# Batch 1's rest ahead of batch 0's main, loads in two column halves from SP's queue, later weight blocks

## The chip, the cores and the metric

The kernel runs on one core of a Trainium2 chip. The metric is the device time of one execution in microseconds (us), lower is better. TensorE is called PE here, VectorE DVE, ScalarE ACT, GpSimd POOL, SyncE SP; PEld is PE's weight load.

## What is computed

A long convolution of 12480 tokens by 128 channels, and two layers of a feed-forward network with 2048 hidden channels behind it, all in float32:

```python
h_filt = (np.maximum(pos_emb @ w1, 0.0) @ w2) * np.exp(-0.01 * pos)[:, None]
u = x * v
y = np.fft.irfft(np.fft.rfft(u, n=2*S, axis=1) * np.fft.rfft(h_filt, n=2*S, axis=0), n=2*S, axis=1)[:, :S]
a = x * y
h = a @ w_in;  a = (h * np.clip(h + 3, 0, 6) / 6) @ w_out        # first layer
h = a @ w_in2; out = where(h > 0, h, exp(min(h, 0)) - 1) @ w_out2 # second layer
```

The four weight matrices arrive as 64-bit floats.

## The kernel before

**Stages.** The convolution is a two-stage Fourier transform written as matrix products, in four steps: `first` (over token blocks), `second` (per frequency, with the product by the filter), `third_main` and `third_rest` (back along one axis) and `fourth` (back along the other, into tokens). The two layers follow as one long stream, called step five here. Every instruction is issued in the order in which the program text calls it, each engine runs its own in that order, and pools and semaphores only add waits; no scheduler moves anything.

**Step three** ends with `third_main(0, ...)`, nine pieces of the main frequencies of channel half 0 (seven of 8 channels, two of 4). For each piece PE makes `q` (L495), ACT copies half of it (L510), DVE adds and subtracts it into `main` (L501). All nine must have left DVE before a matmul of step four may read `main`.

**Step four** has 17 batches (`BATCHES`). `fourth(i, y)` multiplies in two parts: `most` reads `main`, `rest` reads `own` and `other`, which are complete since before `third_main(0, ...)`. Batch 0 has half as many matmuls as the others. Even batches do rest, then most; odd ones most, then rest. DVE then multiplies the result by the signal (L728, L731). Each batch needs a table `ti` (294 KB, six slots, so that batch i+6's is loaded by `load_ti` once batch i has left PE) and a piece of the signal `xT` (`load_x`), brought by SP's DMA queue. `behind` makes a load wait for the last ACT instruction that was noted in `paced`.

**The weights' conversion** runs beside all this. `weight_steps` is a generator of 32 jobs of 256 columns: load 64-bit words (L261), rebuild 32-bit floats with ACT (L271, L272), DVE (L283 to L286) and POOL (L289), and store to `w_scratch` (L266, on ACT's queue). A job's load is issued two steps ahead. In steps one and two the loads go out on SP's queue; `queue[0] = nc.scalar` moves them to ACT's queue from step three on. `convert(RATE[..])` advances the generator at a fractional rate: 0.45 per piece of `third_main(0, ...)`, 0.55 per batch of step four, and `convert(1000)` does what is left after the last batch.

**Step five** reads the converted weights back as 16 blocks of 512 columns, `W[i, q]` (L707), and splits each in two (`split_w`: ACT L711, then POOL or DVE L712) at the unit that `pieces` names. Three blocks are loaded during the last batches of step four, the other 13 in one go after it. A unit n multiplies one 256-column part of the hidden layer for one tile of 512 tokens: `mm1` (L807) makes h in one of three PSUM buffers, ACT activates (L817 or L819), DVE gates (L828 or L830), ACT and DVE split the result (L836, L841), and `mm2` (L851) adds it to the accumulator `acc[m]`, whose buffer has the tag `o1` or `o2` by the layer m. Every unit has 12 PE matmuls; the first layer runs alone for 13 units.

## Time and profile before

| what | value |
|---|---|
| median of 3 timed runs | 1328.4 us (1328.37 to 1329.41) |
| the profiled execution's own time | 1326.08 us |
| its span, first to last instruction | 1324.3 us |
| PE busy in the span | 1313.1 us (99%) |
| DVE, ACT, POOL busy | 1137.3, 1005.5, 406.0 us |
| TensorE's granted clock | 1.000 of full speed |
| start of step four on PE, start of step five on PE | 213.63 us, 252.90 us |

The first five rows are from the list of times and the head of the profile page, the last from the timeline. The span is counted from the first instruction; the profiled execution's own time is 1.8 us longer than its span, for what lies around it. PE is the bound by its share alone, so what can be saved is the time in which it stands still, or work that it does twice.

### The profile page before, as it was taken

To read this page: it belongs to the slowest core of one execution; us is meant where nothing else is said; L and a number is where in the kernel's file an instruction comes from. 1 tells how busy PE (TensorE), PEld (TensorE's weight loads), DVE (VectorE), ACT (ScalarE), POOL (GpSimd) and SP (SyncE) were. 2 spreads that over 40 slices of the span, in tenths; PEclk is the share of its full clock that TensorE was granted. 3 is DMA by queue.
4 is the path that set the end of the run, shared out by engine and by line. 5 is a ranking of instruction groups with operands and counts; after the bars stand their busy time and mean duration, and the time that the engine had idled before them with its cause. 6 is when DMAs were issued, how large, how long until landed. Compare 5 with 4: busy or idle time off the path is not lost.

```text
span 1324.3 us, 22981 instructions
## 1 busy us (share of the span) xinstructions
PE 1313.1 (99%) x9184; PEld 1127.5 (85%) x9184; DVE 1137.3 (86%) x1213; ACT 1005.5 (76%) x1210; POOL 406.0 (31%) x302
## 2 busy tenths in 40 slices
PE   9999999999999999999999999999999999999998
PEld 9999999878888888888888888888888888888898
DVE  6769877699988888888888888888888888898897
ACT  5677663488878887788878887788778878887776
POOL 1027741214222322222233322222222233322223
PEclk9999999999999999999999999999999999999999
DMA  8945338700000000000000000000000000000000
GB/s 271 267 126 160 108 103 273 230 22 1 9 8 1 9 8 8 1 9 8 9 9 0 9 9 8 0 9 8 9 1 9 8 9 1 8 8 9 8 8 13
DMA packets 33676, 58.80 MB, mean 44 GB/s; under 512 B 3962, under 2 KB 10272, under 8 KB 33568
## 3 DMA queue, kind: packets, MB, share of 16 engines
q1 hardware_dynamic: 27232, 50.18, 12.2%
q10 hardware_dynamic: 6336, 7.15, 1.6%
q8 instruction: 72, 1.18, 0.4%
q14 instruction: 36, 0.29, 0.1%
HBM read 46.73 MB, written 10.58 MB: 43 GB/s over the span
## 4 chain that ended last, share of the span: by engine, by line
PE 92%; DVE 3%; ACT 1%; issue 1%; DMA 1%; POOL 0%; SPq 0%; ACTq 0%; DVEq 0%; POOLq 0%
PE o L851 38%; PE h L807 38%; PE pa L395 4%; PE y L651 3%; PE z L467 2%; PE q L495 2%; PE r L448 1%; DVE gs L841 1%; PE h L457 1%; PE pr L349 1%; PE q L531 1%; DVE g L828 1%; DMA cv<-in_mw 0%; DMA w_scratch<-cv 0%; DVE g L830 0%
## 5 line engine op out<-in xcount | busy, mean ns | idle before, releaser
L851 PE MATMUL o<-gs,w 128*128 128x512 f32 (+1 forms) x2400 | 566.0, 384 | 0.7 <-DVE gs L841 0.4
L851 PEld LDWEIGHTS o<-gs,w 128*128 128x128 f32 x2400 | 445.0, 188 | 86.6 <-ACT y L780 0.8
L820 POOL TENSOR_SCALAR a<-a 128x1024 f32<-128x1024 f32 (+1 forms) x200 | 296.2, 1481 | 713.0 <-ACT a L819 712.9
L841 DVE TENSOR_TENSOR gs<-g,gs 128x1024 fp32r<-128x1024 f32 (+1 forms) x400 | 482.8, 1207 | 4.4 <-ACT gs L836 3.4
L836 ACT CAST gs<-g 128x1024 fp32r<-128x1024 f32 (+1 forms) x400 | 410.1, 1025 | 55.0 <-DVE g L828 53.4
L828 DVE SCALAR_TENSOR_TENSOR g<-a,h 128x1024 f32<-128x1024 f32 (+1 forms) x200 | 238.6, 1194 | 114.6 <-ACT a L817 114.6
L807 PE MATMUL h<-xs,w 128*128 128x512 f32 (+1 forms) x1200 | 298.2, 384 | 2.2 <-DVE g L828 2.2
L807 PE MATMUL h<-x,w 128*128 128x512 f32 (+1 forms) x1200 | 298.1, 384 | 0.2 <-DVE g L830 0.2
L819 ACT ACTIVATE a<-h 128x1024 f32<-128x1024 f32 (+1 forms) x200 | 201.3, 1007 | 90.3 <-PE h L807 89.2
L807 PEld LDWEIGHTS h<-xs,w 128*128 128x128 f32 x1200 | 223.1, 188 | 47.4 <-DVE g L828 3.3
L807 PEld LDWEIGHTS h<-x,w 128*128 128x128 f32 x1200 | 223.1, 188 | 43.8 <-ACT gs L836 0.5
L817 ACT ACTIVATE a<-h,bounds 128x1024 f32<-128x1024 f32 (+1 forms) x200 | 218.8, 1094 | 47.6 <-PE h L807 47.3
L830 DVE SCALAR_TENSOR_TENSOR g<-a,h 128x1024 f32<-128x1024 f32 (+1 forms) x200 | 237.4, 1187 | 0.2 <-POOL a L820 0.2
L289 POOL TENSOR_TENSOR cv<-cv 128x256 int32<-128x256 int32 x32 | 23.4, 732 | 126.3 <-DVE cv L286 118.2
L395 PE MATMUL pa<-tab,qb 98*64 98x180 f32 x512 | 41.6, 316 | 0.0
L395 PEld LDWEIGHTS pa<-tab,qb 98*64 98x64 f32 x512 | 37.7, 138 | 2.4
L271 ACT ACTIVATE cv<-cv 128x256 int32<-128x256 uint32 x32 | 14.2, 444 | 22.6 <-DMA cv<-in_mw 18.1
L712 POOL TENSOR_TENSOR w<-w 128x512 fp32r<-128x512 f32 x12 | 17.1, 1436 | 38.4 <-ACT w L711 38.4
L486 POOL TENSOR_TENSOR qb<-qb,bp 128x1024 f32<-128x1024 f32 (+1 forms) x12 | 26.9, 2244 | 3.9 <-DVE bp L481 3.9
L783 ACT COPY y<-o 128x512 f32<-128x512 f32 (+1 forms) x25 | 14.4, 577 | 17.5 <-PE o L851 17.5
L486 POOL TENSOR_TENSOR au<-qb,au 128x1024 f32<-128x1024 f32 (+1 forms) x12 | 26.9, 2242 | 0.5 <-DVE au L481 0.5
L651 PE MATMUL y<-qb 128*64 128x97 f32 (+3 forms) x688 | 24.6, 248 | 0.0
(97 smaller groups left out, 874.5 us busy)
## 6 DMA issues: line engine op xcount, KB each, us to landing
uv<-in_xc SPq DMA_DIRECT2D x32, 196.0 KB
out_T<-y SPq DMA_DIRECT2D x23, 256.0 KB
qb<-in_gm SPq DMA_DIRECT2D x22, 256.0 KB
cv<-in_mw SPq DMA_DIRECT2D x21, 256.0 KB
au<-in_xT SPq DMA_DIRECT2D x16, 268.0 KB
w_scratch<-cv ACTq DMA_DIRECT2D x32, 128.0 KB
w<-w_scratch SPq DMA_DIRECT2D x16, 256.0 KB
cv<-in_vc SPq DMA_DIRECT2D x20, 196.0 KB
```

Of the source, the lines that this page charges most:

```text
L395: nc.tensor.matmul(pa[f * HN:(f + 1) * HN, j, :2 * NK], lhsT=src(j, f), rhs=table[:, f], start=True, stop=True)
L486: nc.gpsimd.tensor_tensor(out=spectrum(hf, k0 + a, n), in0=m1, in1=m2[:, :, :, ::-1], op=ALU.add)
L651: nc.tensor.matmul(y[c * HD:(c + 1) * HD, b, off:off + w], lhsT=lhsT, rhs=rhs[:, H1 - w:], start=(b, c) in fresh, stop=done, skip_group_ch ...
L807: nc.tensor.matmul(h[:, j], lhsT=wslice(2 * m - 2, a, 2 * u + j), rhs=x[:, b], start=i == 0, stop=i == 2)
L817: nc.scalar.activation(a, h, AF.Relu, bias=three)
L819: nc.scalar.activation(a, h, AF.Exp)
L820: nc.gpsimd.tensor_scalar(a, a, 1.0, 0.0, op0=ALU.min, op1=ALU.max)
L828: nc.vector.scalar_tensor_tensor(g, a, 6.0, h, op0=ALU.min, op1=ALU.mult)
L830: nc.vector.scalar_tensor_tensor(g, a, -1.0, h, op0=ALU.add, op1=ALU.max)
L836: nc.scalar.copy(t[:, 0], g)
L841: nc.vector.tensor_tensor(out=t[:, 1], in0=g, in1=t[:, 0].bitcast(F32), op=ALU.subtract)
L851: nc.tensor.matmul(o[:, :WID[t]], lhsT=wslice(2 * m - 1, a, 2 * u + j), rhs=gs[:, b, j], start=u == 0 and j == 0 and i == 0, stop=u == NU ...
```

## The change

It does six things. (1) The parts of a batch become two calls, and batch 1's rest is multiplied right behind batch 0's rest, ahead of batch 0's main part; from batch 2 on even batches do most, then rest, and odd ones rest, then most. (2) From step three on, loads of signal, tables and 64-bit weights are issued as two halves of the columns, and (3) the weights' loads stay on SP's queue. (4) The conversion runs one job ahead of `third_main(0, ...)`, then at its pieces 2, 4 and 6, then at 0.65 per batch, and is complete after the batches without a remainder; the signal's last eight pieces go with batches 0, 1, 3, 4, 6, 7, 9 and 10 in place of 0 to 7. (5) Of the 13 late weight blocks four are loaded at once and nine wait for the activation four units before their split; six splits come one to four units later. (6) The first tile of the first layer is accumulated in the buffer `o2`, all others of that layer in `o1`.

```diff
@@ -250,7 +250,7 @@
 
     JOBS = [(i, c) for i in range(4) for c in range(0, FF, WC)]
 
-    queue, clamp = [nc.sync], [nc.vector]
+    queue, clamp, parts_of = [nc.sync], [nc.vector], [1]
 
     def weight_steps(jobs, raws, es, rs):
         v = nc.vector
@@ -258,7 +258,9 @@
         def load(k):
             if k < len(jobs):
                 i, c = jobs[k]
-                queue[0].dma_start(raws[k % 3].bitcast(I64), moe_w[i][:, c:c + WC])
+                for a in range(0, WC, WC // parts_of[0]):
+                    b = a + WC // parts_of[0]
+                    queue[0].dma_start(raws[k % 3][:, 2 * a:2 * b].bitcast(I64), moe_w[i][:, c + a:c + b])
 
         def store(k):
             if k >= 0:
@@ -294,7 +296,7 @@
         store(len(jobs) - 1)
 
     weights = weight_steps(JOBS, cut(cv, 2 * WC, 3), cut(cv[:, 6 * WC:], WC, 2), cut(cv[:, 8 * WC:], WC, 4))
-    RATE = (0.75, 0.45, 0.55)
+    RATE = (0.75, 0.65)
     due = [0.0]
 
     def convert(n):
@@ -570,7 +572,7 @@
             load_gm0(2 * (o - 1) + GN + n)
     bctx.close()
     lds = cctx.enter_context(tc.tile_pool(name="ldi", bufs=1, reuse_waits="tile"))
-    queue[0] = nc.scalar
+    parts_of[0] = 2
     xp = au[:, :S]
     tis = {}
 
@@ -583,7 +585,11 @@
     def load_ti(i):
         if i < NG:
             tis[i] = slots[i % TB].rearrange("p (j a) -> p j a", a=H1)
-            return nc.sync.dma_start(slots[i % TB][:, :BLOCKS[i] * H1], ti_d[:, FIRST[i]:FIRST[i] + BLOCKS[i]])
+            h = BLOCKS[i] // 2
+            return [
+                nc.sync.dma_start(slots[i % TB][:, a * H1:b * H1], ti_d[:, FIRST[i] + a:FIRST[i] + b])
+                for a, b in ((0, h), (h, BLOCKS[i]))
+            ]
 
     for i in range(2):
         load_ti(i)
@@ -591,11 +597,11 @@
     rests = groups([ET] * 8 + [4, 4])
 
     def load_x(a, b):
-        return nc.sync.dma_start(xp[:, a:b], xT[:, a:b])
-
-    def behind(dma):
+        return [nc.sync.dma_start(xp[:, p:q], xT[:, p:q]) for p, q in ((a, (a + b) // 2), ((a + b) // 2, b))]
+
+    def behind(dmas):
         tc.add_manual_dep(
-            dma.ins, paced[0].ins.name,
+            dmas[0].ins, paced[0].ins.name,
             mybir.DependencyInfo(mybir.DependencyClass.Sync, mybir.DependencyReason.DATA), reason="pace",
         )
 
@@ -621,6 +627,7 @@
         if i < len(xs_a):
             behind(load_x(*xs_a[i]))
     xs_b = pieces_of(XA, AM, 10)
+    xs_c = pieces_of(AM, S, 8)
     qss[1:] = cut(au[:, AW:], 4 * N2, 2)
     for k in range(AHEAD, 8):
         third_main(1, *mains[k])
@@ -630,6 +637,7 @@
             for p, copy in enumerate((nc.scalar.copy, nc.gpsimd.tensor_copy)):
                 copy(other[p * HD:p * HD + KW, o, ms], stage[(1 - p) * HD:(1 - p) * HD + KW, o, ms])
         behind(load_x(*xs_b[k - AHEAD]))
+    convert(1)
     for k, (s0, n) in enumerate(groups([8] * 7 + [4, 4])):
         third_main(0, s0, n)
         if k < 5:
@@ -637,9 +645,10 @@
         if k % 2 and len(tis) < TB:
             assert (len(tis) - 1) * TW <= (s0 + n) * MS
             behind(load_ti(len(tis)))
-        convert(RATE[1])
+        if k in (2, 4, 6):
+            convert(1)
     clamp[0] = nc.vector
-    after = {i: [z] for i, z in enumerate(pieces_of(AM, S, 8))}
+    after = dict(zip((0, 1, 3, 4, 6, 7, 9, 10), xs_c))
     swctx.close()
 
 
@@ -688,9 +697,8 @@
                             rows = slice(b * HD, b * HD + KW)
                             put(b, c, off, w, (own if b == c else other)[rows, o, i, :, t], ti[rows, at + k], done)
 
-        for k, part in enumerate((rest, most) if i % 2 == 0 else (most, rest)):
-            part(k == 1)
-        return widths
+        order = (rest, most) if i % 2 or i == 0 else (most, rest)
+        return [lambda k=k: order[k](k == 1) for k in range(2)], widths
 
     def new_y(i):
         return bank("y", [128, 2, 512], "py" if (len(BATCHES) - 1 - i) % 4 < 2 else "px")
@@ -704,7 +712,7 @@
     x0 = xs[0]
 
     def load_w(i, q):
-        nc.sync.dma_start(W[i, q][:, 1].bitcast(F32), w_dram[i][:, q * WQ:(q + 1) * WQ])
+        return nc.sync.dma_start(W[i, q][:, 1].bitcast(F32), w_dram[i][:, q * WQ:(q + 1) * WQ])
 
     def split_w(i, q, engine=nc.gpsimd):
         w = W[i, q]
@@ -713,12 +721,23 @@
             out=w[:, 1], in0=w[:, 1].bitcast(F32), in1=w[:, 0].bitcast(F32), op=ALU.subtract
         )
 
+    ahead = []
+    for i in range(2):
+        y = new_y(i)
+        ahead.append((y, *fourth(i, y)))
+    for _, parts, _ in ahead:
+        parts[0]()
     for i, banks in enumerate(BATCHES):
-        y = new_y(i)
-        widths = fourth(i, y)
+        if i < len(ahead):
+            y, parts, widths = ahead[i]
+        else:
+            y = new_y(i)
+            parts, widths = fourth(i, y)
+            parts[0]()
+        parts[1]()
         load_ti(i + TB)
-        for z in after.get(i, []):
-            load_x(*z)
+        if i in after:
+            load_x(*after[i])
         if i in (11, 12, 13):
             load_w(*early[i - 11])
         o = START.get((banks[0][0], 1), 0)
@@ -736,8 +755,9 @@
             split_w(*early[i - 13])
         if i == 3:
             nc.vector.tensor_tensor(out=x0[:, 1], in0=xp[:, :TT], in1=x0[:, 0].bitcast(F32), op=ALU.subtract)
-        convert(RATE[2])
-    convert(1000)
+        if i < 15:
+            convert(RATE[1])
+    assert next(weights, "done") == "done"
     cctx.close()
     wp = ctx.enter_context(tc.tile_pool(name="wp", bufs=1, reuse_waits="tile"))
     sb = ctx.enter_context(tc.tile_pool(name="sb", bufs=2, reuse_waits="tile"))
@@ -747,17 +767,23 @@
     later = {}
 
     pieces = {
-        (1, 0): 1, (0, 3): 2, (1, 1): 3, (1, 2): 5, (1, 3): 7, (2, 0): 10, (2, 1): 13, (3, 0): 14, (2, 2): 15,
-        (3, 1): 17, (2, 3): 18, (3, 2): 20, (3, 3): 27,
+        (1, 0): 1, (0, 3): 2, (1, 1): 3, (1, 2): 5, (1, 3): 7, (2, 0): 10, (2, 1): 13, (3, 0): 16, (2, 2): 18,
+        (3, 1): 20, (2, 3): 22, (3, 2): 24, (3, 3): 28,
     }
     splits = {}
-    for (i, q), n in pieces.items():
+    loads = {}
+    for k, ((i, q), n) in enumerate(pieces.items()):
         W[i, q] = wp.tile([128, 2, WQ], F32R, name=f"w{i}_{q}")
-        load_w(i, q)
         splits.setdefault(n, []).append((i, q))
+        if k < 4:
+            load_w(i, q)
+        else:
+            loads.setdefault(n - 4, []).append((i, q))
     def split_at(n):
         for p in splits.get(n, []):
             split_w(*p, nc.vector if 1 < n < 8 else nc.gpsimd)
+        for p in loads.get(n, []):
+            behind([load_w(*p)])
 
     xin = {}
 
@@ -814,7 +840,7 @@
         h = st[n][0]
         a = sb.tile([128, 2, TT], F32, tag="a", name="a", bufs=3)[:, :, :WID[units[n][1]]]
         if m == 1:
-            nc.scalar.activation(a, h, AF.Relu, bias=three)
+            paced[0] = nc.scalar.activation(a, h, AF.Relu, bias=three)
         else:
             nc.scalar.activation(a, h, AF.Exp)
             nc.gpsimd.tensor_scalar(a, a, 1.0, 0.0, op0=ALU.min, op1=ALU.max)
@@ -844,7 +870,7 @@
         m, t, u = units[n]
         gs = st.pop(n)[1]
         if u == 0:
-            acc[m] = po.tile([128, 512], F32, tag=f"o{m}", name=f"o{m}")
+            acc[m] = po.tile([128, 512], F32, tag=f"o{m if t else 2}", name=f"o{m}")
         o = acc[m]
         for j in range(2):
             for i, (a, b) in enumerate(((1, 0), (0, 1), (0, 0))):
```

Where PE's instructions moved: the beginning of step four. `y` is the result, `ti` the tables (1807 is the slot of batch 0, 1808 that of batch 1), `qb` holds `main`, `own` and `other`; L651 before is L660 now. Before:

```order
L495 MATMUL q<-cs,qb 64x64 x256
...
L651 MATMUL y<-ti_1807,qb 64x97 x8
L651 MATMUL y<-ti_1807,qb 64x98 x2
L651 MATMUL y<-ti_1807,qb 64x97 x2
L651 MATMUL y<-ti_1808,qb 64x98 x2
```

and now:

```order
L660 MATMUL y<-ti_1807,qb 64x97 x4
L660 MATMUL y<-ti_1808,qb 64x98 x4
L660 MATMUL y<-ti_1808,qb 64x97 x4
...
L660 MATMUL y<-ti_1807,qb 64x98 x2
L660 MATMUL y<-ti_1807,qb 64x97 x2
L660 MATMUL y<-ti_1808,qb 64x98 x2
```

Of slot 1808, 16 matmuls of batch 1's rest now stand between the two parts of batch 0; before they stood behind batch 1's main.

DVE at the end of step four. `au<-y,au` is the product by the signal (128x390 and 128x98 are the last batch, 128x780 a full one), the rows on `cv` are a job of the weights' conversion, `g` is step five's first gate. Before:

```order
L728 TENSOR_TENSOR au<-y,au 128x780
L731 TENSOR_TENSOR au<-y,au 128x390
L731 TENSOR_TENSOR au<-y,au 128x98
L283 TENSOR_SCALAR cv<-cv 128x256
L285 TENSOR_SCALAR cv<-cv 128x256
L286 SCALAR_TENSOR_TENSOR cv<-cv 128x256
L769 TENSOR_TENSOR xs_3438<-au,xs_3438 128x512
L828 SCALAR_TENSOR_TENSOR g<-a,h 128x1024 x2
```

and now:

```order
L285 TENSOR_SCALAR cv<-cv 128x256
L287 TENSOR_SCALAR cv<-cv 128x256
L288 SCALAR_TENSOR_TENSOR cv<-cv 128x256
L747 TENSOR_TENSOR au<-y,au 128x780 x2
L750 TENSOR_TENSOR au<-y,au 128x390
L750 TENSOR_TENSOR au<-y,au 128x98
L795 TENSOR_TENSOR xs_3490<-au,xs_3490 128x512
L854 SCALAR_TENSOR_TENSOR g<-a,h 128x1024 x2
```

The last job of the conversion stood behind the last batch's product and now stands ahead of the products of the last three batches.

SP's queue in the first batches of step four, with what each issue waits for (DMAHW0 to DMAHW7 are the eight counters of landed DMAs, which all DMAs of SP and ACT take in turn; an issue that names one waits for the landing of the DMA that had it before). Before:

```order
L586 DMA ti_1807<-in_ti 128x588 [waits DMAHW4_49,PE_49]
L594 DMA au<-in_xT 128x488 [waits DMAHW5_49,Pool_49]
L586 DMA ti_1808<-in_ti 128x588 [waits DMAHW7_49,PE_49]
L594 DMA au<-in_xT 128x488 [waits DMAHW0_49,Pool_49]
L586 DMA qb<-in_ti 128x588 [waits DMAHW2_49,PE_49]
```

and now:

```order
L590 DMA ti_1807<-in_ti 128x294 [waits DMAHW6_49,PE_49]
L590 DMA ti_1807<-in_ti 128x294 [waits DMAHW7_49]
L600 DMA au<-in_xT 128x244 [waits DMAHW0_49,Pool_49]
L600 DMA au<-in_xT 128x244 [waits DMAHW1_49,Pool_49]
L590 DMA ti_1808<-in_ti 128x294 [waits DMAHW2_49,PE_49]
L590 DMA ti_1808<-in_ti 128x294 [waits DMAHW3_49,PE_49]
L600 DMA au<-in_xT 128x244 [waits DMAHW4_49]
L600 DMA au<-in_xT 128x244 [waits DMAHW5_49,Pool_49]
L263 DMA cv<-in_mw 128x128 [waits DMAHW6_49,DVE_49]
L263 DMA cv<-in_mw 128x128 [waits DMAHW7_49]
```

Each load has become two, and the weights' loads (`cv<-in_mw`), which ACT issued before, stand among them.

## Rows read from the trace of the kernel before

**Rows 1.** Busy time by stretch: us of each engine (instructions), clock, DMA share, GB/s.

```profile
253.00:266.00 13.00, 11.30 (x49) 9.00 (x50) 10.51 (x14) 9.95 (x13) 2.17 (x3) 1.00 0.77 242
266.00:298.00 32.00, 31.16 (x135) 24.85 (x134) 32.00 (x29) 27.48 (x33) 6.63 (x5) 1.00 0.04 15
298.00:1324.30 1026.30, 1022.46 (x4619) 856.16 (x4617) 903.13 (x817) 816.91 (x869) 301.47 (x204) 1.00 0.02 7
```

**Rows 2.** Timeline of PE, 195 to 300 us: start, length, instruction [idle before, releaser].

```profile
213.63 0.57 PE L651 MATMUL y<-ti,qb 52*64 52x97 f32 x16
215.75 3.08 PE L651 MATMUL y<-ti,qb 128*64 128x97 f32 x80 [1.55 <-DVE qb L501]
218.65 9.00 PE L651 MATMUL y<-qb 52*64 52x98 f32 x256
...
244.05 2.73 PE L651 MATMUL y<-ti,qb 128*64 128x98 f32 x71 [0.78 <-issue]
...
252.90 4.40 PE L807 MATMUL h<-xs,w 128*128 128x512 f32 x18
258.99 3.01 PE L807 MATMUL h<-xs,w 128*128 128x512 f32 x12 [1.70 <-DVE g L828]
...
284.42 1.66 PE L851 MATMUL o<-gs,w 128*128 128x512 f32 x6 [0.36 <-ACT y L780]
...
297.43 1.67 PE L807 MATMUL h<-xs,w 128*128 128x512 f32 x6 [0.48 <-DVE g L828]
```

**Rows 3.** Timeline of ACT and DVE at the end of step three.

```profile
213.00 0.47 ACT L271 ACTIVATE cv<-cv 128x256 int32<-128x256 uint32 x1 [0.79 <-DMA cv<-in_mw]
...
213.76 0.43 DVE L286 SCALAR_TENSOR_TENSOR cv<-cv 128x256 int32<-128x256 int32 x1
213.88 0.37 ACT L510 COPY tab<-q 128x256 f32<-128x256 f32 x1
...
214.28 0.76 DVE L501 TENSOR_TENSOR qb<-q,tab 128x256 f32<-128x256 f32 x2
214.95 0.75 DVE L501 TENSOR_TENSOR qb<-q,au 128x256 f32<-128x256 f32 x2
```

**Rows 4.** Timeline of the DMA issues on ACT's and SP's queues.

```profile
207.75 0.34 ACTq L261 DMA_DIRECT2D cv<-in_mw  x1
...
216.69 0.33 SPq L586 DMA_DIRECT2D ti<-in_ti  x1
...
217.11 0.38 SPq L594 DMA_DIRECT2D au<-in_xT  x1
```

**Rows 5.** DMA from 215 to 240 us: queue (q1 SP, q10 ACT), packets, MB, share.

```profile
DMA packets 4581, 7.96 MB, mean 318 GB/s; under 512 B 501, under 2 KB 2309, under 8 KB 4575
...
q1 hardware_dynamic: 2721, 5.29, 61.4%
q10 hardware_dynamic: 1854, 2.58, 33.0%
```

**Rows 6.** Timeline of all engines at the start of step five.

```profile
251.91 4.09 ACTq L266 DMA_DIRECT2D w_scratch<-cv  x2
...
254.88 0.74 POOL L289 TENSOR_TENSOR cv<-cv 128x256 int32<-128x256 int32 x1 [1.76 <-DVE cv L286]
256.05 0.62 ACT L767 CAST xs<-au 128x512 fp32r<-128x512 f32 x1 [7.44 <-PE h L807]
256.57 2.11 ACT L817 ACTIVATE a<-h,bounds 128x1024 f32<-128x1024 f32 x2
...
257.71 2.35 DVE L828 SCALAR_TENSOR_TENSOR g<-a,h 128x1024 f32<-128x1024 f32 x2 [0.32 <-ACT a L817]
258.58 0.62 ACT L711 CAST w<-w 128x512 fp32r<-128x512 f32 x1
...
260.19 1.47 DVE L841 TENSOR_TENSOR gs<-g,gs 128x1024 fp32r<-128x1024 f32 x1
```

**Rows 7.** Timeline of SP's queue: the first late weight block.

```profile
253.04 0.32 SPq L707 DMA_DIRECT2D w<-w_scratch  x1
```

## Prediction

> **What bounds the kernel now.** I read the busy time by stretch first, then PE's timeline, then each place where PE stands still. From 298 us to the end PE is busy for 1022.46 of 1026.30 us [rows 1], with no wait worth a row, and nothing is changed there. So the change can only take away or add time in which PE waits, from the end of step three to 298 us. PE's timeline names five such places [rows 2]: 1.55 us ahead of batch 0's main part, where DVE releases it; 0.78 us in step four, where no semaphore releases it ("issue"); 1.70 us behind the first three units of step five; 0.36 us for an accumulator; 0.48 us for a gate. The sum, 4.87 us, is the most that could be gained; it is 0.37% of the median. The profiled execution took 1326.08 us, 2.3 us under the median of the timed runs, so I take differences on the former and subtract them from the latter. About 0.2%, or 2.7 us, is what a measurement of this kernel can tell from no change.
>
> **Batch 1's rest ahead of batch 0's main.** PE ends batch 0's rest at about 214.2 us and stands until 215.75 [rows 2], because DVE writes the last pieces of `main` until 214.95 + 0.75 = 215.70 us [rows 3]. The 16 matmuls that now come first need nothing from those pieces. Four batches take 9.00 us [rows 2], so one takes 2.25 and half of one 1.1 us. They fill 1.1 of the 1.55 us. Is the end of `main` moved? ACT's copies started at 213.88, late, because a conversion step had waited 0.79 us for its weights at 213.00 [rows 3]. That step stands at the same place in the change. DVE also has a conversion instruction there (213.76 + 0.43 = 214.19 us) just ahead of 214.28, so even earlier copies would win only 0.1 us. I take **1.1 us** (0 if the copies get later by that much, 1.55 if `main` is also earlier).
>
> **The start of step five.** PE does three units from 252.90 to 257.29 us and then waits 1.70 us for the first gate [rows 2]: there are three buffers for h. ACT could have activated unit 0 when its matmuls ended, a third of 4.40 us after 252.90, near 254.4. It starts at 256.57, because two stores of converted weights stand ahead of it from 251.91 for 4.09 us; the second needs POOL's result of 254.88 + 0.74 = 255.62 us [rows 6]. (The row of the cast at 256.05 names PE, which had long been done; the stores are what ended last.) In the change the last conversion stands ahead of the last three products on DVE, some 5 us earlier, so its store finds POOL done. Then ACT: cast from 252.9 to 253.5, activation 254.4 to 255.5 (2.11 us for two [rows 6]), gate 1.2 us (2.35 for two) to 256.7, ahead of 257.29. The wait is gone, provided that weight block (1, 0) is there when ACT casts it, near 256.8 now. Its load is issued at 253.04 [rows 7]; it has landed by 258.58, where ACT takes it without a wait [rows 6], and may have landed any time before. Behind it the chain is 5.1 us from the first activation to the split result (256.57 to 260.19 + 1.47), so 259.5 now, ahead of PE, which needs it at about 257.3 + 2 x 1.4 = 260.1. I take **1.6 us** (0 to 1.70).
>
> **The smaller waits.** The wait of 0.36 us ends when ACT has emptied the first tile's accumulator [rows 2]. The second tile gets another buffer, and the second layer's first output asks for the old one much later: **0.36 us** (0 to 0.36). The 0.48 us fall into a stretch in which DVE is busy 32.00 of 32.00 us [rows 1]; it starts 1.9 us earlier against PE's 1.7, and three splits that POOL and ACT did around there come later: **0.3 us** (-0.5 to 0.48; bunched splits elsewhere could cost as much). The 0.78 us without a releaser stand in step four, while DMA is nearly full: q1 and q10 together had a share of 94.4% from 215 to 240 us [rows 5]. Bytes hardly change; the signal's loads are spread over more batches. I take half, **0.4 us** (-0.8 to 0.78).
>
> **The loads.** Moving the weights' loads takes 0.34 us per issue [rows 4] off ACT, which is idle there: nothing. On SP the issues follow each other in 0.42 us (216.69 to 217.11 [rows 4]). Batches 0 to 10 issue 11 pairs of tables, 8 of signal and 7 of weights, 52 issues or 21.8 us, while PE needs 11 x 2.2 = 24.2 us for these batches: it fits, with a tenth to spare. The eight counters allow eight DMAs in the air. With some 8 stores among them that is 60 DMAs, 7.5 rounds of eight; PE's pace asks for 24.2 / 7.5 = 3.2 us from issue to landing. A full load took 213.00 - 207.75 = 5.25 us [rows 3, 4], when eight loads of about 250 KB could be in the air. With halves of about 135 KB it is 1.08 MB, 3.4 us at the 318 GB/s of this stretch [rows 5]. So SP falls behind by about 1.5 us over the step, and a table that is asked for six batches ahead has 5 x 2.2 = 11 us before it is needed, less 3.4: 7.6 us of slack. I cost it at **0** (0 to 9 us, below). Deferring nine weight blocks moves DMA into a stretch with a share of 0.04 [rows 1]; a block asked for four units (10.9 us) ahead of its split has twice the 5.25 us: nothing.
>
> Sum: 1.1 + 1.6 + 0.36 + 0.3 + 0.4 = 3.76 us, taken as 3.8. 1328.4 - 3.8 = **1324.6 us**.
>
> The Trainium skill (*DMA: Bandwidth & Descriptors*, "Bandwidth") speaks against the halves: "Batch DMAs to ≥1 MiB for ≥75% of peak", with 341 GB/s at 1 MB and 138 at 64 KB. By that table the halves would sink far under the 318 GB/s that loads of 128 to 294 KB reach here with several in the air [rows 5], and rival one below would be the outcome; that the present loads, all under a third of its size, already come near its rate says that it describes a DMA alone. No row here shows one alone.
>
> **Rival one: the halves make DMA slower, and step five starts as late as before.** On q10, 2.58 MB in 1854 packets take 33.0% of sixteen engines for 25 us, 71 ns for 1391 bytes; on q1 it is 90 ns for 1944 [rows 5]. A line through both has 23 ns per packet and 0.0345 ns per byte, so a packet of 972 bytes costs 57 ns, 1.26 times as much per byte. With 8 of 10 bytes halved, the 8.0 MB of batches 0 to 10 then need about 30.5 us at 263 GB/s, 6.3 us more than PE's 24.2. The slack of 7.6 us just covers the tables, but the last conversion gets late again and the 1.6 us are lost, or block (1, 0) lands late with the same effect. Gain 2.1, **1326.3 us**. For it: the two packet costs. Against it: they mix loads and stores, and queues that take turns.
>
> **Rival two, slower: SP's queue falls behind.** If a half takes as long from issue to landing as a full load now, 5.25 us [rows 3, 4], the 7.5 rounds need 39.4 us, 15.2 more than PE; less the slack (11 - 5.25) PE stands 9.4 us in step four for tables that were asked for too late. With the 1.6 us at step five gone too and only 1.5 us kept, it is 1328.4 + 7.9 = **1336.3 us**. It decides from a landing time of 4.6 us: 8.5 x 4.6 - 35.2 = 3.9, less 1.5, is about the 2.7 us that can be told. For it: 5.25 us is what the trace shows, and one queue in order holds tables behind weights that wait for DVE. Against it: with half the bytes in the air, the wait for a turn on nearly full engines should halve.
>
> **How the numbers follow.** Forecast 0.66, of which 0.06 is a gain under 2.7 us; rival one 0.20; rival two 0.14, of which 0.12 is slower by over 2.7 us and 0.02 within. Faster 0.60, same 0.28, slower 0.12. The bottom of the range takes in all five waits (1323.5) and 1 us of scatter between runs: 1322.5. The top takes in rival one and the mild end of rival two, 1329.5; above it lies less than 0.1.
>
> **What would show it.** In the changed profile: the wait ahead of batch 0's main near 0.4 us; the wait behind the first three units of step five gone, with ACT's first activation near 1.5 us behind PE's first matmul there; none for the accumulator. Wrong would be PE waiting for DMA (tables) in step four, SP's table issues later than the batch that frees their slot by several us, or ACT behind a weight block.

## The result and the profile after

The changed kernel takes **1338.65 us** (median of 4 runs, 1335.59 to 1339.33) where the kernel before took 1328.38 beside it: a ratio of 1.0074, 95% interval 1.0062 to 1.0087. It is 10.3 us slower. The profiled execution took 1338.86 us, its span is 1337.1 us (before 1324.3), the mean granted clock 0.994 (1.000). Times by stretch below are differences of the two profiled executions.

PE's timeline of the changed kernel, where it stands still or runs slowly; it answers [rows 2]:

```profile
215.05 1.24 PE L660 MATMUL y<-ti,qb 52*64 52x97 f32 x48 [1.00 <-issue]
219.23 4.16 PE L660 MATMUL y<-ti,qb 128*64 128x97 f32 x48 [2.94 <-DVE qb L503]
...
252.81 3.25 PE L660 MATMUL y<-qb 52*64 52x98 f32 x84 [0.15 <-DMA qb<-in_ti]
256.64 1.22 PE L660 MATMUL y<-qb 128*64 128x98 f32 x28 [0.59 <-DMA qb<-in_ti]
263.91 9.74 PE L833 MATMUL h<-xs,w 128*128 128x512 f32 x30 [6.05 <-POOL w L720]
...
313.16 1.66 PE L833 MATMUL h<-xs,w 128*128 128x512 f32 x6 [0.30 <-DVE g L854]
330.48 1.66 PE L833 MATMUL h<-xs,w 128*128 128x512 f32 x6 [0.70 <-DVE g L854]
```

The two waits that the change was to shorten are longer: 2.94 us ahead of batch 0's main part (1.55) and 6.05 us ahead of step five's first matmul (none there before, 1.70 three units later). Only 0.74 us are waits for tables. The waits shown sum to 11.73 us, against 4.87 before [rows 2]: 6.9 of the 12.8 us of span. The rest is in the length of the rows behind the two long waits, and the windows of PE in the changed kernel show why (time, PE busy and matmuls, granted clock, DMA share, GB/s):

```profile
220.00:222.00 2.00, 2.00 (x28) 0.50 0.32 92
222.00:224.00 2.00, 2.00 (x30) 0.50 0.87 258
224.00:226.00 2.00, 2.00 (x46) 0.72 0.90 256
226.00:228.00 2.00, 2.00 (x78) 1.00 0.81 233
...
264.00:266.00 2.00, 2.00 (x5) 0.50 0.95 344
266.00:268.00 2.00, 2.00 (x6) 0.50 0.07 24
268.00:270.00 2.00, 2.00 (x7) 0.62 0.00 0
270.00:272.00 2.00, 2.00 (x10) 1.00 0.00 0
```

Behind each of the two waits PE ran at 1.2 GHz, half its clock, for 5.9 and 5.6 us, which cost 2.9 us (219.23 to 226: 0.5 x 4.77 + 0.28 x 2) and 2.8 us (263.91 to 270: 0.5 x 4.09 + 0.38 x 2). So 6.9 + 5.7 = 12.6 us, and the account closes.

What PE waited for is on ACT and SP. ACT, with one row of DVE (217.75), in the changed kernel:

```profile
216.40 0.43 ACT L273 ACTIVATE cv<-cv 128x256 int32<-128x256 uint32 x1 [3.48 <-DMA cv<-in_mw]
217.35 0.37 ACT L512 COPY tab<-q 128x256 f32<-128x256 f32 x1
217.75 0.76 DVE L503 TENSOR_TENSOR qb<-q,tab 128x256 f32<-128x256 f32 x2 [2.14 <-ACT tab L512]
...
258.89 0.43 ACT L273 ACTIVATE cv<-cv 128x256 int32<-128x256 uint32 x1 [3.57 <-DMA cv<-in_mw]
261.89 0.62 ACT L719 CAST w<-w 128x512 fp32r<-128x512 f32 x1 [2.12 <-DMA w<-w_scratch]
```

Both chains begin with a conversion step that waits for its 64-bit weights: 3.48 us ahead of the last copies of `main` (0.79 before [rows 3]), 3.57 us ahead of the cast of step five's first weight block, which then waits another 2.12 us for that block. Those loads are late because SP issues them late (start, length, issues of one line in a row):

```profile
211.19 0.85 SPq L263 DMA_DIRECT2D cv<-in_mw  x2
...
220.83 0.81 SPq L590 DMA_DIRECT2D ti<-in_ti  x2
221.73 0.86 SPq L600 DMA_DIRECT2D au<-in_xT  x2
...
232.14 2.32 SPq L600 DMA_DIRECT2D au<-in_xT  x2
...
248.81 2.55 SPq L600 DMA_DIRECT2D au<-in_xT  x2
...
256.64 5.56 SPq L715 DMA_DIRECT2D w<-w_scratch  x6
```

The 64-bit load that ended ACT's wait at 216.40 went out from 211.19 on; the one that ended ACT's wait at this place before was issued by ACT at 207.75 [rows 4]. That is 3.44 us later, and batch 0's main part begins 3.48 us later (219.23 against 215.75). From 220.83 to the first early weight block (L715) SP issues 52 loads in 35.8 us. A pair without a wait follows the next in 0.9 to 1.0 us, 0.48 us an issue: 25 us; about 10 us more lie in the long rows. The kernel before issued its first early block (L707) 17 us sooner (e3 below, without the loads' edits, 12.5 us sooner):

```profile
234.52 5.01 SPq L586 DMA_DIRECT2D qb<-in_ti  x3
239.59 22.61 SPq L707 DMA_DIRECT2D w<-w_scratch  x14
```

DMA itself was not fuller. The list of queues from 217 to 257 us (packets, MB, share of sixteen engines), first the changed kernel, then the one before:

```profile
q1 hardware_dynamic: 7458, 7.16, 63.5%
q10 hardware_dynamic: 1152, 1.05, 7.7%
```

```profile
q1 hardware_dynamic: 3562, 6.83, 52.0%
q10 hardware_dynamic: 2475, 3.18, 24.4%
```

71% in place of 76% of the engines' time, for 8.2 MB in place of 10.0. The Trainium skill (*Perfetto Trace Analysis*, "What 'DMA-bound' means") lists the sequencer of the issuing engine, a track that is solid with issues, as a bound of its own beside the DMA engines. SP's rows above and the falling share agree with it.

### The profile page after: what moved, and what is told of

It is laid out like the page before. It is cut to its first block, busy times and chain, and to the rows that moved or that the text cites. A ratio compares the mean times of both kernels' runs of the same rounds, so it can differ in the third digit from the quotient of the medians.

```text
span 1337.1 us, 23090 instructions
## 1 busy us (share of the span) xinstructions
PE 1318.5 (99%) x9184; PEld 1131.0 (85%) x9184; DVE 1137.7 (85%) x1213; ACT 1005.5 (75%) x1210; POOL 408.7 (31%) x302
## 3 DMA queue, kind: packets, MB, share of 16 engines
q1 hardware_dynamic: 36304, 53.07, 12.8%
## 4 chain that ended last, share of the span: by engine, by line
PE 88%; DVE 4%; issue 3%; ACT 2%; DMA 1%; POOL 1%; SPq 0%; ACTq 0%; DVEq 0%; POOLq 0%
PE h L833 37%; PE o L877 36%; PE pa L397 4%; PE z L469 2%; PE y L660 2%; DVE gs L867 2%; PE q L497 1%; PE r L450 1%; PE h L459 1%; PE pr L351 1%; PE q L533 1%; DVE g L854 1%; DMA cv<-in_mw 1%; ACT a L843 0%; DMA w<-w_scratch 0%
## 5 line engine op out<-in xcount | busy, mean ns | idle before, releaser
L846 POOL TENSOR_SCALAR a<-a 128x1024 f32<-128x1024 f32 (+1 forms) x200 | 299.5, 1497 | 701.0 <-ACT a L845 701.0
L285 DVE TENSOR_SCALAR cv<-cv 128x256 f32<-128x256 f32 x28 | 17.3, 619 | 19.3 <-ACT cv L274 19.3
```

Of the source, the lines that this page charges most:

```text
L846: nc.gpsimd.tensor_scalar(a, a, 1.0, 0.0, op0=ALU.min, op1=ALU.max)
```

## The experiments

Theories at the start: one, the count, which is twice as many issues at 0.48 us in one ordered queue with eight DMAs in the air; two, the order, in which weights' loads stand in SP's queue behind loads that wait; three, small packets. From e11 on the recorded texts call a loss in proportion to the number of DMAs theory one, and a threshold of SP's queue, with the loop of e13, theory two.

**Which of the loads' two edits: e1, e2, e3.** All three keep everything else of the change. e1 takes the halves back, e2 gives the weights' loads back to ACT's queue, e3 does both.

e2:

```diff
     parts_of[0] = 2
+    queue[0] = nc.scalar
```

e1 (e3 has both edits):

```diff
-    parts_of[0] = 2
+    parts_of[0] = 1
...
-        return [nc.sync.dma_start(xp[:, p:q], xT[:, p:q]) for p, q in ((a, (a + b) // 2), ((a + b) // 2, b))]
+        return [nc.sync.dma_start(xp[:, a:b], xT[:, a:b])]
```

and `load_ti` likewise.

> The change with whole loads again (one DMA each for signal, tables and weights), all still on SP's queue. Theory one (count: twice as many issues at about 0.48 us each in one ordered queue, eight in the air, make every load late): the loads are back in time, 1325 to 1327 us, no idle of PE over 1 us at the start of step five. Theory two (order: weights' loads in SP's queue stand behind loads that wait for PE or for a store's landing, halves or not): still 1332 us or more, with ACT waiting over 20 us for cv<-in_mw. Theory three (small packets move fewer bytes per second): 1325 to 1327 us as well.

> The change with halves kept, but the weights' loads of steps three and four on ACT's queue as before. Theory one (count): SP has 14 issues fewer, ACT 22 more; most of the loss stays or half of it, 1331 to 1338 us. Theory two (order): the weights come in time again, 1325 to 1328 us. Theory three (packets): nothing changes, 1337 to 1340 us.

> The change without halves and with the weights' loads on ACT's queue: what is left is batch 1's rest ahead, the conversion's schedule, the late weight blocks and the accumulator. All theories: the forecast's sum of about 3.8 us, 1324 to 1326 us; if it is 1328 or more, those parts bring nothing.

Measured: e1 1329.47 us (ratio to before 1.0010, 0.9996 to 1.0025), e2 1330.23 (1.0023, 1.0008 to 1.0037), e3 1328.05 (1.0001, 0.9989 to 1.0012). Neither edit alone does the damage: against e3, SP's queue costs 1.4 us, halves 2.2, both 10.6. No theory forecast this: e1 lies above the range of one and three (1325 to 1327) and below that of two (1332), e2 between one (from 1331) and two (to 1328). e2 issues the same DMAs, with the same packets and the same eight counters as the change; only 14 of the 52 issues are on another queue, and 8.4 us are gone. That speaks against small packets and against the number of DMAs in the air, and for the issues in SP's one queue. PE's rows of e3 show what is left of the forecast without the loads:

```profile
218.59 2.24 PE L657 MATMUL y<-ti,qb 128*64 128x97 f32 x48 [0.70 <-DVE qb L503]
242.67 2.57 PE L657 MATMUL y<-qb 52*64 52x97 f32 x70 [1.92 <-issue]
...
303.16 1.65 PE L830 MATMUL h<-xs,w 128*128 128x512 f32 x6 [0.31 <-DVE g L851]
320.48 1.65 PE L830 MATMUL h<-xs,w 128*128 128x512 f32 x6 [0.71 <-DVE g L851]
```

**Packet size: e4.** Halves by 64 partitions in place of columns, so that packets keep their length.

```diff
-                nc.sync.dma_start(slots[i % TB][:, a * H1:b * H1], ti_d[:, FIRST[i] + a:FIRST[i] + b])
+                nc.sync.dma_start(slots[i % TB][p:p + 64, :BLOCKS[i] * H1], ti_d[p:p + 64, FIRST[i]:FIRST[i] + BLOCKS[i]])
```

> The change with halves cut by partitions (64 rows of full width) in place of columns: as many DMAs as in the change, packets as long as before. Theory one (count): as slow as the change, 1336 to 1341 us. Theory three (packets): 1325 to 1329 us. Theory two (order): as slow as the change.

Measured: 1343.57 us (1.0113, 1.0094 to 1.0132), above the ranges named: full packets do not bring the time back, so theory three falls. SP's rows of e4 (same columns as above) show 1.19 us for a pair in place of 0.86:

```profile
234.12 1.19 SPq L263 DMA_DIRECT2D cv<-in_mw  x2
235.39 1.20 SPq L589 DMA_DIRECT2D qb<-in_ti  x2
```

A pair follows the next in 1.27 us, and the first early block goes out at 262.73. A dearer issue, a later SP and a slower kernel go together here; that a load of 64 partitions is otherwise as quick as one of 128 no run shows.

**How many issues: e12, e11, e16, e17.** Halves for some kinds alone, all on SP's queue: weights (e12), tables (e11), signal (e16), tables and weights (e17).

> The changed kernel with halves for the 64-bit weights alone; tables and signal whole, all on SP's queue: 33 issues in batches 0 to 10. Theory two (threshold on SP's queue): 33 x 0.48 = 15.8 us fit: 1329.5 to 1331.5, a little worse than the tables' halves only where ACT waits for the second half. Theory one (in proportion to the number): 7 of 30 additional issues, 1331 to 1332. Theory three (by bytes, 1.8 of 7.0 MB): 1331 to 1332. Together with the tables alone this tells a threshold (both near 1330) from a loss in proportion (the two losses add up with the signal's to 9 us).

> The changed kernel with halves for the tables alone; signal and weight loads whole, all on SP's queue: 37 issues in batches 0 to 10 in place of 52. Theory two (SP's queue, a threshold where its issues, 0.48 us each, with the waits for stores no longer fit into PE's 24.2 us): 37 x 0.48 = 17.8 us fit, so nearly the time of the whole loads on SP's queue, 1329.5 to 1331. Theory one (in proportion to the number of DMAs): 15 of 30 additional issues are left out and half of the loss between whole (1329.5) and halves (1338.7) stays: 1333 to 1335. Theory three (small packets, in proportion to the bytes in halves, here 3.2 of 7.0 MB): 1333 to 1334.

> The changed kernel with halves for the signal alone; tables and 64-bit weights whole, all on SP's queue: 34 issues in batches 0 to 10. The tables' halves alone gave 1331.2 and the weights' alone 1327.6, where whole loads on this queue gave 1329.5. Theory two (threshold where SP's issues, 0.48 us each, with its waits no longer fit): 34 x 0.48 = 16.3 us fit: 1328 to 1331.5. Rival: the signal's halves, of which sixteen more stand in step three ahead of the tables, are the whole loss by themselves: 1336 or more, with 2 us or more of wait ahead of batch 0's main part.

> The changed kernel with halves for tables and 64-bit weights, the signal whole, all on SP's queue: 44 issues in batches 0 to 10 (52 in the change, 26 with whole loads; 33 gave 1327.6, 34 gave 1332.9 and 37 gave 1331.2). Threshold (SP's time from the first freed table to the first early block must stay under some 28 us; at 0.48 us an issue and 10 us of waits 44 take 31): 1332 to 1334, less than the sum of the steps to the full loss. In proportion: 1329.5 + 18/26 x 9.2 = 1335.9. If the sum of the two kinds alone holds (+1.7 - 1.9): 1329.3.

Measured: e12 1327.58 us (ratio 0.9993, 0.9980 to 1.0005), e11 1331.23 (1.0017, 1.0003 to 1.0032), e16 1332.91 (1.0034, 1.0016 to 1.0053), e17 1332.15 (1.0038, 1.0026 to 1.0051). With the other kernels in which SP's queue differs, in the order of the first early block's issue (the runs of before beside these have medians of 1327.70 to 1328.51):

| kernel | issues of SP, batches 0 to 10 | first early block issued, us | PE's wait for DVE ahead of batch 0's main | PE's wait ahead of step five | median, us |
|---|---|---|---|---|---|
| before | 19 | 239.59 | 1.55 | none | 1328.4 |
| e3 | 19 | 244.12 | 0.70 | none | 1328.05 |
| e12, weights | 33 | 244.12 | none | none | 1327.58 |
| e1, whole | 26 | 249.46 | none | none | 1329.47 |
| e16, signal | 34 | 250.78 | none | 4.76 | 1332.91 |
| e11, tables | 37 | 250.99 | none | 3.88 | 1331.23 |
| e2, weights on ACT | 38 | 251.22 | 1.59 | 2.56 | 1330.23 |
| e17, tables and weights | 44 | 251.49 | 0.36 | 4.05 | 1332.15 |
| e13, stores on POOL | 52 | 254.14 | 1.99 | 1.30 | 1332.36 |
| after | 52 | 256.64 | 2.94 | 6.05 | 1338.65 |
| e4, 64 partitions | 52 | 262.73 | 2.35 | 4.69 | 1343.57 |

In proportion to the issues e17 would be 1335.9; it is 1332.15. The three kinds alone cost 3.4 (signal), 1.8 (tables) and -1.9 us (weights) against e1, 3.3 together; at once they cost 9.2. So the costs do not add up. That fits a threshold, but where it would lie these runs do not tell, and the count alone does not set it: e16 with 34 issues missed its 1331.5, e12 with 33 lies under its 1329.5 and is not told from before. What the column on batch 0's main adds: with all loads on SP's queue and at least one kind whole this wait is at most 0.36 us; with halves of all three it is 1.99 to 2.94, and the clock falls behind it. Of the 6.5 us between e17 and the change, 2.6 of wait and 2.9 of clock stand at this place. I did not settle why the signal's halves delay SP more than the weights'.

**Stores behind the same counters: e13.** The stores of converted weights go out on POOL's queue, with counters of their own.

```diff
-                nc.scalar.dma_start(w_dram[i][:, c:c + WC], rs[k % 4])
+                (nc.gpsimd if parts_of[0] == 2 else nc.scalar).dma_start(w_dram[i][:, c:c + WC], rs[k % 4])
```

> The changed kernel, but from step three on the stores of converted weights are issued by POOL, on its own queue and its own set of counters, so that the eight counters of SP's loads are no longer shared with stores. Same loads, same halves, same places in SP's queue. Theory two (a loop: SP's issue waits for the landing of an ACT store that had its counter before, that store stands behind an ACT conversion instruction, which waits for a weight load that stands further back in SP's queue): the long issues of SP (1.0 to 2.1 us, six of them) go, and most of the 10.3 us with them: 1329 to 1332, with less than 1.5 us of wait at step five's first matmul (6.05 now). Theory one (the number of DMAs in the air): 52 loads in 6.5 rounds of eight in place of 7.5, so an eighth of the loss at most: 1337 to 1339. Theory three (small packets): the packets are the same, 1338 to 1340.

Measured: 1332.36 us (1.0028, 1.0018 to 1.0037), 6.3 us less than the change and just outside theory two's range. SP's 52 issues take 31.8 us (222.32 to 254.14) in place of 35.8. SP's waits for a store in the change (204 to 270 us; total, times, longest; 0.6 us of the second row lies ahead of 220.83), and one single issue:

```profile
SPq L600 <- DMA w_scratch<-cv: 1.7, 2, 1.0
SPq L590 <- DMA w_scratch<-cv: 1.2, 2, 0.6
```

```profile
249.29 2.07 SPq L600 DMA_DIRECT2D au<-in_xT  x1
```

In e13 no wait of SP for a store is left. So the loop is real: SP waits for the landing of a store, ACT issues that store behind a conversion, and the conversion waits for a load further back in SP's queue. Its waits are 2.3 us of those 35.8; without them SP is 4.0 us quicker. But theory two's own sign fails: the six long issues (in the change 1.04 to 2.07 us each, 9.3 us together, where one without a wait takes 0.33 to 0.44) are still there, with 0.66 to 2.82 us each and 8.2 together. What holds them stays open: the list of SP's waits names PE for 0.9 and 0.8 us in two of the change's six, and nothing of that size in the others. In this execution PE's wait ahead of step five is 1.30 us and the granted clock behind it 1.00, so the 2.8 us of half clock at this place are gone too; ahead of batch 0's main 1.99 us of wait and half clock behind it stay. The edit also takes the stores, with their waits for POOL, out of ACT's order, so not all of the 6.3 us need be the counters'. The loop is part of the cause, not all of it.

**Where the delay is collected: e18.** The three early blocks are loaded from POOL's queue, at batches 6 to 8 (`load_w` takes the queue as an argument).

```diff
-        if i in (11, 12, 13):
-            load_w(*early[i - 11])
+        if i in (6, 7, 8):
+            load_w(*early[i - 6], nc.gpsimd)
```

> The changed kernel with the three early weight blocks loaded from POOL's queue at batches 6 to 8 in place of SP's at batches 11 to 13; all halves and all other loads stay in SP's queue, as late as they were. Theory: the loss is collected at the first early block, the last kind of load that SP reaches (issued at 256.64, before at 239.59). Then PE's wait of 6.05 us ahead of step five and the half clock behind it (2.4 us) go, and 1338.7 becomes 1330 to 1332; what stays is the wait ahead of batch 0's main with its own half clock (2.94 + 2.8 - 1.55). Rival: the next late loads in SP's queue (the last tables, block (1, 0)) take over as the wait: 1334 or more, with PE waiting for qb<-in_ti or for POOL's split of a later block.

Measured: 1337.99 us (1.0070, 1.0053 to 1.0087). My theory missed by 6 us: the block itself is not what counts. The time is in the rival's range (1334 or more), but hardly for its reason: PE waits 0.82 us for tables, and 4.44 us for the split of step five's first block. ACT in e18:

```profile
256.48 0.43 ACT L273 ACTIVATE cv<-cv 128x256 int32<-128x256 uint32 x1 [4.93 <-DMA cv<-in_mw]
...
260.18 0.43 ACT L273 ACTIVATE cv<-cv 128x256 int32<-128x256 uint32 x1 [2.78 <-DMA cv<-in_mw]
...
261.30 0.62 ACT L719 CAST w<-w 128x512 fp32r<-128x512 f32 x1 [0.24 <-issue]
```

The block was there, but its cast (L719) stands on ACT behind two conversions that wait for 64-bit loads in SP's queue, and is only 0.6 us earlier than in the change (261.89). The early block's issue time in the table is a clock hand for how late SP is; the delay is collected wherever ACT or PE meets a late load. In the change the cast stands behind a conversion that could begin at 258.89 and then waits 2.12 us for its block; in e18 the block's wait is gone, but that conversion begins at 260.18, so one late load is left where there were two.

**What the clock costs: e10.** 26 matmuls into a buffer that nothing reads keep PE busy through the wait ahead of step five.

```diff
+    fill = pp.tile([128, 2, 512], F32, tag="h", name="fill")
+    for k in range(26):
+        nc.tensor.matmul(fill[:, k % 2], lhsT=x0[:, 0, :128], rhs=x0[:, 0], start=True, stop=True)
```

> The changed kernel with 26 additional matmuls on PE (128x128 by 128x512, about 0.24 us each at full clock, 6.1 us in all) between the last batch of step four and step five's first matmul, into a buffer of h that nothing reads. They fill the 6.05 us in which PE waits for the first weight block and change no load. Theory: the clock fell to half because PE stood still, and that costs 9.74 - 7.1 = 2.6 us for the first 30 matmuls of step five. Then the granted clock stays near 1.00 from 258 to 270 us and the time falls by 1.5 to 2.6 us, to about 1336.5 (a wait for the first gate may take some of it back). Rival: the slow matmuls are hidden, since the gates and the second weight block would make PE wait there anyway: 1338 to 1339.5. Rival: the clock falls for another reason than PE's standing still: the additional matmuls run at half clock too, take up to 12 us, and the time rises to 1343 or more.

Measured: 1336.96 us (1.0063, 1.0048 to 1.0078), 1.7 less than the change, as forecast, though the two intervals overlap; the rows tell more than the time. PE's timeline, and a window, of e10:

```profile
257.71 6.19 PE L898 MATMUL fill<-xs 128*128 128x512 f32 x26
263.74 7.07 PE L833 MATMUL h<-xs,w 128*128 128x512 f32 x30
```

```profile
264.00:266.00 2.00, 2.00 (x10) 1.00 0.50 180
```

The loads are as late as ever, but the same 30 matmuls take 7.07 us in place of 9.74, at 2.4 GHz. The 2.7 us of this row are the price of the clock at this place; that it does not fall when PE is kept busy shows that the standing still made it fall.

**Batch 1's rest alone, and before once more: e5, e8.** e5 is the kernel before with only the rest moved (the hunks of `fourth` and of the batch loop).

> The kernel before with one part of the change alone: batch 1's rest ahead of batch 0's main part. No load, queue, conversion or split is touched. Theory: PE's wait ahead of batch 0's main falls from 1.55 to about 0.45 us, all other waits stay: 1.1 us less than before, 1327.2 where before has 1328.3, hardly to be told from it. Rival: the new order of batch 1 makes the first tables or accumulators late: a new wait in the first batches, 1328.3 or more.

> The kernel before, unchanged, once more with a profile. In the first profile PE stood 0.78 us in step four where no semaphore released it (the releaser reads issue); in the changed kernel with the old loads it was 3.81 us. Theory: these waits are scatter from one execution to the next, which makes up the spread of before's own times (1325.7 to 1331): the time of this execution differs from 1326.1 by about as much as the sum of these waits does. Rival: they belong to the changed order, and this profile shows 0.8 us again whatever its time.

Measured: e5 1328.96 us (1.0006, 0.9995 to 1.0016; one more execution took 7054.60 us and is not in the ratio), no gain; e8 1328.39 us in one execution. PE in e5, then a window of it, then PE in e8:

```profile
215.98 2.83 PE L651 MATMUL y<-ti,qb 52*64 52x97 f32 x66 [1.17 <-issue]
...
227.02 3.89 PE L651 MATMUL y<-qb 52*64 52x97 f32 x67 [1.66 <-issue]
...
252.45 4.41 PE L651 MATMUL y<-qb 52*64 52x97 f32 x120 [1.39 <-issue]
```

```profile
228.00:230.00 2.00, 2.00 (x27) 0.50 1.00 331
```

```profile
217.56 3.07 PE L651 MATMUL y<-ti,qb 128*64 128x97 f32 x80 [1.58 <-DVE qb L501]
236.15 7.34 PE L651 MATMUL y<-qb 128*64 128x98 f32 x197 [0.30 <-issue]
246.18 2.74 PE L651 MATMUL y<-ti,qb 128*64 128x98 f32 x71 [0.78 <-issue]
```

In e5 the wait for DVE ahead of batch 0's main is gone altogether (1.55 before), but 1.17 us without a releaser stand in the same stretch, so this profile does not show what the rest alone fills. All waits without a releaser sum to 4.2 us, and behind one of 1.66 us the clock was halved. In e8, the same program as before, these waits sum to 2.3 us (1.2 of them in step three) where the first profile had 0.78, and its time is 2.3 us longer. So they scatter between executions of one program, and a gain of 1 us in one stretch does not show against them. In e1 to e3 and e5 they come only in steps three and four, with 2.7 to 5.0 us in all; in the rows of e1 and e3 the next one often stands 127 matmuls behind the last. They stand at fixed places: counted from the start of the trace through PE's instructions, weight loads included, each of them in all sixteen profiles is instruction 193 or 194 of a group of 256, but for the wait named last below, and the 0.78 us of before, the 0.78 of e8 and the 0.93 of e1 are the same instruction. So what scatters is how long PE stands at these places, not where. That PE's instructions are loaded there in blocks is a guess that no run tests. The one of another kind stands at step four's first matmul, 1.00 us in the change (215.05) and 0.55 to 2.02 in e2, e4, e10, e13 and e18; no kernel with a whole kind of load has it, so it belongs to the halves.

**A version a little under before: e15.** The change with halves for the weights alone (e12), and the nine late blocks split at their old places.

```diff
-(3, 0): 16, (2, 2): 18, (3, 1): 20, (2, 3): 22, (3, 2): 24, (3, 3): 28,
+(3, 0): 14, (2, 2): 15, (3, 1): 17, (2, 3): 18, (3, 2): 20, (3, 3): 27,
```

> Candidate: the changed kernel with halves for the 64-bit weights alone, and with the nine late weight blocks split at their old places (four units later than their load, as in the change). The later places had cost 0.3 + 0.66 us of gate waits in place of 0.48. Expected from the weights' halves alone: 1327.6 - 0.5 = 1327.1, 1.2 us or 0.1% under before, at the edge of what can be told. If the second gate wait has another cause, 1327.6.

Measured: **1325.38 us** (12 runs; before 1327.70 beside it), ratio 0.9985, 0.9974 to 0.9997: under before by 2.3 us, which the interval just tells from nothing and which is less than the 2.7 us that the prediction asks for; under the change by 13. PE's timeline of e15:

```profile
216.62 2.24 PE L656 MATMUL y<-ti,qb 128*64 128x97 f32 x48 [0.19 <-DVE qb L503]
248.39 4.41 PE L656 MATMUL y<-qb 52*64 52x97 f32 x120 [0.71 <-issue]
252.73 7.19 PE L829 MATMUL h<-xs,w 128*128 128x512 f32 x30
...
295.62 1.66 PE L829 MATMUL h<-xs,w 128*128 128x512 f32 x6 [0.57 <-DVE g L850]
```

0.19 us ahead of batch 0's main, none at step five, none for the accumulator, one gate wait: this is nearly the profile that I had forecast, and nearly the time (1324.6). Its gain over e12 was expected at 0.5 us and came out at 2.2; the gate waits account for 0.4 of it (0.30 + 0.66 to 0.57), and the rest I put down to scatter, which is not shown.

## Why the prediction was wrong, point by point

**The failed step** is "I cost it at **0**" for the loads. Three things were wrong in it.

- *The issues.* "In 0.42 us ... it fits, with a tenth to spare" took one pair of rows. Back to back it is 0.48 us, which makes 25 us, more than PE's 24.2, before any wait. Some 10 us come on top: 2.3 of waits for stores, which ACT issues late because SP is late, some 2 in which SP stands until PE frees a table's slot, and about 7 by which six single issues took longer than the others (1.04 to 2.07 us), for a reason that stays open.
- *The slack.* I worked it out for the tables, "7.6 us", which is nearly right: PE lost only 0.74 us to them. But SP's queue also held the 64-bit loads, behind which ACT's copies, casts and stores stand in order. They had no such slack: 3.44 us of delay at 211.19 came back as 3.48 us at 219.23, where batch 0's main begins, and the last of them set the cast for step five (e18).
- *The price of standing still.* I counted a wait as its own length. Two of them cost 2.9 and 2.8 us more, at half the clock (e10: 2.7 us in one row). In [rows 2] no wait was longer than 1.70 us and the mean granted clock was 1.000, so those rows had no price for it; I should have named it as unknown.

**Rival two** is the nearest: SP's queue falls behind. But it has SP wait for landings, and of the 35.8 us only 2.3 are such waits that a view names; the issues themselves are the larger part. In the one pair that can be followed its landing time held (the second half of the pair at 211.19, issued at 211.62, ended ACT's wait at 216.40: 4.8 us, above its point of decision at 4.6). Its place was wrong (PE "for tables that were asked for too late"), and its price of 1336.3 came near 1338.65 only because the clock's 5.7 us, which it left out, stand where it had put too long a wait for tables. Its chance of 0.14 was too low: the 5.25 us that it took for a half was the only landing time in the rows, and the 3.4 us that I preferred was an estimate.

**Rival one**, small packets, is not the cause. A packet costs 93 ns for 1917 bytes before and 54 ns for 960 now, 1.17 times as much per byte (1.26 forecast), but the engines were less busy, not more, and e4 with full packets is slower.

**The five waits**, as e3 shows them without the loads. Term one: 1.55 to 0.70 us, 0.85 gained of 1.1; in e15 1.36, but 0.24 us without a releaser stand just ahead of it. It was over-sized: I took half a batch's time for batch 1's rest, but batch 0's rest and it together take 1.24 us (the row at 215.05) where batch 0's alone took 0.57 [rows 2], so it fills 0.67. Term two: 1.70 to nothing, right at 1.6 and for its reason: ACT's first activation in e3 starts 1.69 us behind PE's first matmul of step five (258.07 and 256.38; 1.5 forecast). Term three: 0.36 to nothing, right. Term four had the wrong sign: 0.48 us became 0.31 + 0.71; with the late splits at their old places it is 0.57 (e15). Term five was mis-sized: the waits without a releaser were 0.78 us in the one profile that I had, of an execution 2.3 us under the median; e8, at the median, has 1.5 us more of them. They are not the change's to halve: 3.81 us in e3 and 4.2 in e5, and the 3.0 us that e3 has more than before outweigh the 2.4 us that the other four terms gave.

## What to carry to other kernels

When transfers move to another queue or are cut up, write that queue out in order with its measured time per issue and the counters that it shares, and ask for each consumer, not for one kind of load, how late it may come; an engine that runs in order behind one late load makes all its later work late. A wait of TensorE that is longer than those in the trace at hand can cost more than its length, since the work behind it may run at half the clock: here 2.9 us more behind 2.94 and 2.8 more behind 6.05. Before promising a gain of a microsecond or two, look at several profiles of the same program for waits that scatter.

## What was not expected of the hardware

- A load of 64 partitions took SP longer to issue than one of 128 with half the columns: 1.27 against 0.95 us for a pair (230.22 to 231.17 in the change).
- TensorE's clock fell to 1.2 GHz behind waits of 2.94 and 6.05 us, and in e5 behind one of 1.66 us; behind e3's 1.92 us and the 1.30 us of e13 ahead of step five it stayed at 1.00. The Trainium skill (*TensorE: Matmul & The Clock Gate*, "What's actually happening") has an idle TensorE at 1.2 GHz; the falls here agree with it. Which of such short waits do it, these rows do not tell.
- Waits of PE without a releaser come to between 0.5 us (e12) and 5.0 us (e1) in an execution, all while the loads run, and but for those at step four's first matmul each at instruction 193 or 194 of a group of 256.
- Single issues of SP took 1.04 to 2.07 us, six of 52 in the change, where most take 0.33 to 0.44; in before and e3, with 19 issues in these batches, the longest took 0.73 and 0.74.
